# Four column tiles for three matrix-vector products of an attention and MLP training step

## The chip, the cores and the metric

One core of one Trainium2 chip runs the whole program in one launch. The metric is the device time of a run in microseconds (us), as a median over runs; lower is better. TensorE multiplies matrices (PE in the profile, PEld for its weight loads), VectorE (DVE) and ScalarE (ACT) work on rows and copy results out of PSUM, GpSimd (POOL) and SyncE (SP) here mostly issue transfers.

## The reference

One token, x of 1 x 1024, goes twice through attention and an MLP with the same weights, and then all gradients are computed with a given gradient of the output:

```
def _A_ref(x, k_cache, v_cache, wq, wo):        # 32 heads, 4 kv groups, head size 128, last 4096 positions
    q = (x @ wq).reshape(...)                   # wq 1024 x 4096
    p = softmax(q k^T * 128**-0.5)
    return (p v).reshape(B, Sq, 4096) @ wo      # wo 4096 x 1024
def _B_ref(x, w1, b1, w2):
    h = x @ w1 + b1                             # w1 1024 x 3584
    act = h * tanh(softplus(h))
    return act @ w2                             # w2 3584 x 1024
x = x + A(layernorm(x)); x = x + B(layernorm(x))
x = x + A(layernorm(x)); x = x + B(layernorm(x))
```

The outputs are x and the gradients of the first x, both caches, wq, wo, w1, b1 and w2, all bf16. The gradients of the caches (1 x 4 x 32768 x 128 each) are zero outside the last 4096 positions, and these zeros are written too.

## The kernel before

Vectors of 1024, 3584 or 4096 numbers are held as columns: 128 partitions by 8, 28 or 32 columns. A weight matrix comes from memory in chunks of 1 MB, in the slots of a ring of eight (`Ring`; `want` queues a load, `release` frees a slot and lets SP issue the next load that was wanted, `lend` adds slots). A forward product takes 128 x 128 blocks of a chunk as the stationary operand and one column of the vector as the moving operand, and adds up columns in PSUM. Backward products need the transposed matrix: TensorE transposes eight blocks at a time into a PSUM bank (`turn_pe`, L452), ACT or DVE copies them back over the chunk (`turn_ev`, `evac`, L305 and L308), and then the same form of product follows, put off by `later` until two or more such groups are under way (`mv`, L471). Part of the rows is done instead by DVE as dot products (`rowdot`, L429).

The order, with l = 0 and 1 for the two layers of each kind: attention 0, MLP 0, attention 1 (`attn_fwd`), the first half of MLP 1 (`mlp_fwd`); then backward through MLP 1 (`dn_b1`), attention 1 (`attn_bwd`), MLP 0, attention 0; at the end the outer products of the weight gradients and the cache gradients are computed and stored (`work`). The second MLP's output is not needed until the end, so its product with w2 (`mlp_out`, L697) is done on the way back, in the loop over w2's seven chunks in which the gradient of the first MLP also passes through w2 (`rows_chunk`). Engines follow the program's order; nothing is rescheduled.

What the change touches:

- In `attn_fwd`, the loop over wo's eight chunks (L596), 32 matmuls for each, with `wo_hook` after each chunk. In the second layer the hook does one `conv`: eight transposes of a block of the K cache and a copy, work for the backward pass. The result goes to `residual` (L387), and from there through a layernorm to the MLP.
- In `mlp_fwd`, the loop over w1 (L645), 224 matmuls, whose result `h_ps` goes to DVE (L658). W1 stays in SBUF.
- The loop over w2's chunks on the way back (from L1094), with `mlp_out` ahead of `rows_chunk`. Here a row group is transposed in two of four, and DVE takes the other two. After it follow `dn_b0`, which ends with `ring.lend`, and `attn_bwd(0, ...)`, whose hooks `do1(c)` run after each wo chunk.
- PSUM: SC0 and SC1, MV, TP and three BIG banks. Seven of eight banks are in use.

The zeros of the cache gradients go out as 56 transfers of 1 MB. `zeros(n, after)` issues n of them on POOL at points in the program that were chosen by hand; a tiny copy of `after` makes POOL wait until that value exists.

Of the kernel before, what the change touches and what calls it, by code (L numbers as in the profile page):

```python
# [9 lines left out]
FP32 = mybir.dt.float32  # L10
BF16 = mybir.dt.bfloat16
ACT = mybir.ActivationFunctionType
ALU = mybir.AluOpType
AX = mybir.AxisListType

P = 128
HQ = 32
# [6 lines left out]
TD = D // P  # L24
TF = F // P
# [68 lines left out]
def kernel(  # L94
# [22 lines left out]
    nc = tc.nc  # L117
# [10 lines left out]
    psum = way.enter_context(tc.tile_pool(name="psum", bufs=1, space=bass.MemoryType.PSUM))  # L128
    dram = ctx.enter_context(tc.tile_pool(name="dram", bufs=1, space=bass.MemoryType.DRAM))

    def sb(shape, dtype, name):
        return keep.tile(shape, dtype, name=name)
# [12 lines left out]
    W1 = sb([P, TD, F], BF16, "W1")  # L145
# [8 lines left out]
    small = junk[:].bitcast(FP32)  # L154

    mlp_t = DSX[:, 0:1024].bitcast(FP32)
# [4 lines left out]
    SC = [psum.tile([P, 512], FP32, name=f"SC{i}")[:] for i in range(2)]  # L161
    MV = psum.tile([P, 512], FP32, name="MV")
    TP = psum.tile([P, 512], FP32, name="TP")
    bigs = [psum.tile([P, 512], FP32, name=f"BIG{i}")[:] for i in range(3)]
    big_n = [0]

# [22 lines left out]

    spread = sb([P, P + 3], BF16, "spread")  # L190
    nc.vector.memset(spread[:], 0.0)
    quarter = sb([P, 4], FP32, "quarter")
    nc.vector.memset(quarter[:], 0.0)
    for hi in range(4):
# [6 lines left out]
    NB = sb([P, TD, 2], BF16, "NB")  # L201
    GA = sb([P, TD, 2], BF16, "GA")
    GB = sb([P, TD, 2], BF16, "GB")
    OC = sb([P, HQ, 2], BF16, "OC")
    DQC = sb([P, HQ, 2], BF16, "DQC")
    AC = sb([P, TF, 2], BF16, "AC")
# [13 lines left out]
    ring = Ring(nc, [ring_t[:, i, :] for i in range(8)])  # L220
# [115 lines left out]
    def f_block(row, b):  # L336

        c = b // 4
        return row[:, 512 * c:512 * (c + 1)].rearrange("a (p k) -> a k p", k=4)[:, b % 4, :]

    def into_fours(dst, col):

# [40 lines left out]
    def residual(y_ps, x, name):  # L383
        xn = sb([P, TD], FP32, f"x_{name}")
        st = tmp([P, 2], FP32, "st")
        junk = tmp([P, TD], FP32, "xx")
        nc.vector.scalar_tensor_tensor(out=xn[:], in0=y_ps, scalar=1.0, in1=x[:], op0=ALU.mult, op1=ALU.add,  # L387
                                       accum_out=st[:, 0:1])
        nc.vector.scalar_tensor_tensor(out=junk[:], in0=xn[:], scalar=1.0, in1=xn[:], op0=ALU.mult, op1=ALU.mult,
                                       accum_out=st[:, 1:2])  # L390
        return xn, st
# [110 lines left out]
    def attn_fwd(l, x, st, first, wo_hook, q_hook=None):  # L502
        name = f"A{l}"
# [7 lines left out]
        for k, t in enumerate(order):  # L511
            ch = ring.get(("q", l, t))
            for h in range(HQ):
                nc.tensor.matmul(q_ps[:, h:h + 1], lhsT=ch[:, h * P:(h + 1) * P], rhs=NA[:, t, l:l + 1],  # L514
                                 start=(k == 0 and h == 0), stop=(k == TD - 1), skip_group_check=True)
# [11 lines left out]
        for i in range(2):  # L527
            for t in range(16 * i, 16 * i + 16):
                for g in range(G):
                    c = scol(g, t) - 512 * i  # L530
                    nc.tensor.matmul(SC[i][:, c:c + 8], lhsT=KT[:, g, t, :],
                                     rhs=QC[:, 0, g * 32 + l * 8:g * 32 + l * 8 + 8], start=True, stop=True)
            nc.vector.reduce_max(m64[i][:], SC[i].rearrange("p (tp c) -> p c tp", c=64), axis=AX.X)
        if not first:
# [5 lines left out]
                                op=ALU.max)  # L540
# [20 lines left out]
        for i in range(2):  # L561
            nc.vector.reduce_sum(m64[i][:], EX[:, i * 512:(i + 1) * 512].rearrange("p (tp c) -> p c tp", c=64), axis=AX.X)
            for g in range(G):
                for t in range(16 * i, 16 * i + 16):
                    c = scol(g, t)
# [24 lines left out]
        y_ps = MV[:, 128:128 + TD]  # L590
        for c in range(8):
            ch = ring.get(("o", l, c))
            for tt in range(4):
                h = 4 * c + tt
                for dd in range(TD):
                    nc.tensor.matmul(y_ps[:, dd:dd + 1], lhsT=ch[:, tt, dd * P:(dd + 1) * P], rhs=OC[:, h, l:l + 1],  # L596
                                     start=(h == 0 and dd == 0), stop=(h == HQ - 1), skip_group_check=True)
            if first:
                ring.release(("o", l, c))
            wo_hook(c)  # L600
        xn, stn = residual(y_ps, x, name)
        return xn, stn, dict(n32=n32, rstd=rstd, o32=o32)

# [34 lines left out]
    def mlp_fwd(l, x, st, mid):  # L638
        name = f"B{l}"
        n32, rstd = ln_fwd(x, st, NB[:, :, l], name)  # L640
        mid()
        h_ps = MV[:, 192:192 + TF]
        for t in range(TD):
            for fb in range(TF):
                nc.tensor.matmul(h_ps[:, fb:fb + 1], lhsT=f_block(W1[:, t], fb), rhs=NB[:, t, l:l + 1],  # L645
                                 start=(t == 0 and fb == 0), stop=(t == TD - 1), skip_group_check=True)

        taken = []

        def col(n):  # L650
            if n == "mp":
                return sb([P, TF], FP32, f"{n}_{name}")
            taken.append(n)
            return mlp_t[:, (len(taken) - 1) * TF:len(taken) * TF]

        h, nh, z, w, m, om, A, B, num, den, t_, = (col(n) for n in "h nh z w m om A B num den t".split())
        V = nc.vector
        V.tensor_tensor(out=h[:], in0=h_ps, in1=b1c[:], op=ALU.add)  # L658

        V.scalar_tensor_tensor(out=nh[:], in0=h[:], scalar=-1.0, in1=h[:], op0=ALU.mult, op1=ALU.min)  # L660
        nc.scalar.activation(z[:], nh[:], ACT.Exp)
        nc.scalar.activation(w[:], nh[:], ACT.Exp, scale=2.0)
        V.tensor_scalar(out=m[:], in0=h[:], scalar1=0.0, scalar2=None, op0=ALU.is_ge)
        V.tensor_scalar(out=om[:], in0=h[:], scalar1=0.0, scalar2=None, op0=ALU.is_lt)
        V.tensor_tensor(out=A[:], in0=m[:], in1=w[:], op=ALU.max)
        V.tensor_tensor(out=B[:], in0=om[:], in1=w[:], op=ALU.max)
        V.scalar_tensor_tensor(out=num[:], in0=z[:], scalar=2.0, in1=A[:], op0=ALU.mult, op1=ALU.add)
        V.scalar_tensor_tensor(out=den[:], in0=B[:], scalar=2.0, in1=num[:], op0=ALU.mult, op1=ALU.add)
        V.reciprocal(den[:], den[:])
        V.tensor_tensor(out=t_[:], in0=num[:], in1=den[:], op=ALU.mult)  # L670
        if l == 0:
            V.tensor_tensor(out=AC[:, :, l], in0=h[:], in1=t_[:], op=ALU.mult)

        def deriv():

            mp, sg, s2 = col("mp"), col("sg"), col("s2")
            V.tensor_scalar(out=s2[:], in0=z[:], scalar1=1.0, scalar2=None, op0=ALU.add)
            V.reciprocal(s2[:], s2[:])
            V.tensor_tensor(out=sg[:], in0=m[:], in1=z[:], op=ALU.max)
            V.tensor_tensor(out=sg[:], in0=sg[:], in1=s2[:], op=ALU.mult)  # L680
            V.tensor_tensor(out=mp[:], in0=t_[:], in1=t_[:], op=ALU.mult)
            V.tensor_scalar(out=mp[:], in0=mp[:], scalar1=-1.0, scalar2=1.0, op0=ALU.mult, op1=ALU.add)
            V.tensor_tensor(out=mp[:], in0=mp[:], in1=h[:], op=ALU.mult)
            V.tensor_tensor(out=mp[:], in0=mp[:], in1=sg[:], op=ALU.mult)
            V.tensor_tensor(out=mp[:], in0=mp[:], in1=t_[:], op=ALU.add)
            return mp

        def act_late():
            V.tensor_tensor(out=AC[:, :, l], in0=h[:], in1=t_[:], op=ALU.mult)

        return dict(n32=n32, rstd=rstd, deriv=deriv, act_late=act_late)

    def mlp_out(l, ch, c, y_ps):
        for tt in range(4):
            fb = 4 * c + tt
            for dd in range(TD):
                nc.tensor.matmul(y_ps[:, dd:dd + 1], lhsT=ch[:, tt, dd * P:(dd + 1) * P], rhs=AC[:, fb, l:l + 1],  # L697
                                 start=(fb == 0 and dd == 0), stop=(fb == TF - 1), skip_group_check=True)
# [326 lines left out]
    def units_rows(base, nblk, out):  # L1025

        for c in range(nblk // 4):
            s = stage_free.popleft()
            for tt in range(4):
                n = 0  # L1030
                while n < 2:
                    m = unit_dw(base, NOFF + (4 * c + tt) * P, 512 * n, s[:, tt * D + n * 512:(tt + 1) * D], 2 - n)
                    n += m
                    store(out.rearrange("(c p k) d -> p c (k d)", p=P, k=4)[:, c], s, 2 * tt + n - m, 2 * tt + n, 8,
                          c == nblk // 4 - 1)
                    yield
# [64 lines left out]
    bigs.append(SC[1])  # L1101
    for c in range(7):
        ch = ring.get(("2", 1, c))
        mlp_out(1, ch, c, y_ps)
        flush()
        rows_chunk(ch, c, GB, 0, LB[0], da0, DA, 2 if c else 0, "A" if c else None, ("2", 1, c))
        later(lambda c=c: ring.release(("2", 1, c)))
        if c in (2, 4):
            zeros(1, da0[:, 4 * c:4 * c + 1])
# [9 lines left out]
    nc.vector.tensor_copy(GA[:, :, 0], g1[:])  # L1119

    x4 = sb([P, TD], BF16, "x4")
    nc.vector.tensor_tensor(out=x4[:], in0=y_ps, in1=x3[:], op=ALU.add)
    db = sb([P, TF], BF16, "db")
    nc.vector.tensor_tensor(out=db[:], in0=dh0[:], in1=dh1[:], op=ALU.add)

# [5 lines left out]
    def do1(c):  # L1131
        if c == 0:
            rowize(GA, TD, 32, 0)
        if c == 3:
            todo[1].append(units_rows(32, HQ, out_5))
        if c == 5:
            store_rows(x4[:], TD, out_0[0, 0, :])
            store_f(db)
        if c == 5:
            zeros(2, do1_acc[:, 4 * c:4 * c + 1])  # L1140
# [76 lines left out]
```

## Time and profile before

| | |
|---|---|
| median of 3 runs | 457.55 us (455.9 to 457.78) |
| profiled execution | 456.82 us, of which the span from first to last instruction is 455.0 us |
| mean granted TensorE clock | 0.641 |
| busy share of the span | PE 72%, PEld 58%, DVE 57%, ACT 46%, POOL 9% |
| DMA | 181.48 MB (81.84 MB read, 98.62 MB written from the HBM's side), mean 399 GB/s |
| attention 1, output product (L596) | 133.15 us to 145.99 us, when `residual` starts |
| MLP 1, first product (L645) | 149.16 us to 159.69 us, when its result is read |
| w2's loop on the way back | 252.25 us to 277.44 us |

Times inside the execution count from the start of the span. The page cuts the span into 40 equal slices and gives each engine's busy share as a digit in tenths; the line PEclk is the clock that the throttle granted to TensorE, in tenths of full speed with 9 for 90% or more; the line GB/s is what all DMA queues moved. A timeline line has start, length, engine, source line, operation, output and input, count, and in brackets the idle time before it with what ended it. Matmuls are pipelined: the length of a group of matmuls runs from the first start to the modelled end of the last.

### The profile page before, as it was taken

What the parts mean: (1) busy time and instruction counts of PE and PEld (TensorE: products, weight loads), DVE (VectorE), ACT (ScalarE), POOL (GpSimd) and SP (SyncE); (2) the same over time, 40 slices, a digit from 0 to 9 for tenths busy, and PEclk for the clock granted to TensorE, in tenths of its full rate; (3) what the DMA queues carried; (4) which work ended last, traced back from release to release, by engine and by line L of the source; (5) the groups of instructions that cost most, each with busy time, mean ns of one, the idle gap of its engine ahead of it and who ended that gap; (6) DMA issues with size and microseconds to landing.
All of it is one profiled execution on the core that took longest, in us unless ns stands there. A gap on an engine that the chain in (4) does not pass through costs nothing. (4 is left out here: it accounts for less than half of the span.)

```text
span 455.0 us, 14050 instructions
## 1 busy us (share of the span) xinstructions
PE 326.4 (72%) x6289; PEld 262.1 (58%) x6289; DVE 258.8 (57%) x508; ACT 210.6 (46%) x245; POOL 38.8 (9%) x86
## 2 busy tenths in 40 slices
PE   3836543456599788898797988798977898889500
PEld 3735443456598778797797877796861222235300
DVE  4504747277450075477366847486377999888600
ACT  2501001011055276687066452283349999999500
POOL 1000000002032221200210101012221000000000
PEclk9955555555555588999589655697675555555555
DMA  8999999989989999999999899999999999999996
GB/s 336 424 418 418 421 416 419 419 321 421 421 349 403 401 407 412 410 393 418 420 419 421 341 402 333 361 371 416 421 420 420 417 421 423 423 419 419 404 408 248
DMA packets 28091, 181.48 MB, mean 399 GB/s; under 512 B 3675, under 2 KB 3703, under 8 KB 9463
## 3 DMA queue, kind: packets, MB, share of 16 engines
q1 hardware_dynamic: 19874, 121.84, 66.1%
q0 software_dynamic: 8064, 58.72, 31.6%
q8 instruction: 49, 0.80, 0.7%
q14 instruction: 12, 0.09, 0.0%
q10 hardware_dynamic: 92, 0.02, 0.0%
HBM read 81.84 MB, written 98.62 MB: 397 GB/s over the span
## 5 line engine op out<-in xcount | busy, mean ns | idle before, releaser
L308 ACT COPY ring<-BIG 128x1024 bf16<-128x1024 bf16 x51 | 50.5, 1015 | 44.0 <-PE BIG L452 37.6
L1019 PE MATMUL wide<-W 2*128 2x512 bf16 x228 | 52.1, 598 | 9.3 <-ACT W L308 2.0
L452 PE MATMUL BIG<-ident_bf,ring 128*128 128x128 bf16 x664 | 55.5, 238 | 1.4 <-ACT ring L308 0.4
L452 PEld LDWEIGHTS <-ring 128*128 128x128 bf16 x768 | 53.2, 109 | 2.4 <-issue 1.7
L429 DVE CUSTOM_DVE_ANT_0 junk<-ring,SC 128x1024 bf16<-128x1024 bf16 x32 | 38.9, 1215 | 6.7 <-DMA ring<-in_B_w_dram 6.2
L1019 PEld LDWEIGHTS <-W 2*128 2x128 bf16 x240 | 12.6, 102 | 44.3 <-issue 43.2
L471 PEld LDWEIGHTS <-ring 128*128 128x128 bf16 x864 | 29.9, 97 | 10.5 <-issue 6.8
L305 DVE CAST ring<-wide 128x1024 bf16<-128x1024 f32 (+1 forms) x29 | 33.7, 1200 | 3.2 <-PE wide L1019 1.5
L308 ACT COPY KT<-BIG 128x1024 bf16<-128x1024 bf16 x22 | 21.9, 1011 | 27.5 <-PE BIG L625 26.0
L308 ACT CAST ring<-wide 128x1024 bf16<-128x1024 f32 (+1 forms) x35 | 32.9, 1018 | 1.3 <-PE wide L1070 0.5
L305 DVE COPY ring<-BIG 128x1024 bf16<-128x1024 bf16 x32 | 21.8, 689 | 16.6 <-PE BIG L452 12.7
L264 POOL DMA_DIRECT2D out_dram<-zt x56 | 29.7, 534 | 15.0 <-DMA out_dram<-zt 14.2
L429 DVE CUSTOM_DVE_ANT_0 junk<-ring,DSX 128x1024 bf16<-128x1024 bf16 x24 | 29.4, 1224 | 0.8
L645 PE MATMUL MV<-NB,W 128*128 128x1 bf16 x448 | 16.5, 172 | 15.5 <-DMA W<-in_B_w_dram 12.7
L645 PEld LDWEIGHTS <-W 128*128 128x128 bf16 x448 | 15.8, 118 | 16.3 <-DMA W<-in_B_w_dram 13.4
L452 PE MATMUL BIG<-ident_bf,W 128*128 128x128 bf16 x288 | 23.3, 227 | 2.4 <-issue 2.4
L514 PE MATMUL MV<-NA,ring 128*128 128x1 bf16 x512 | 15.2, 165 | 13.1 <-DMA ring<-in_A_wq_dram 11.8
L308 ACT COPY W<-BIG 128x1024 bf16<-128x1024 bf16 x21 | 20.6, 1015 | 7.9 <-PE BIG L452 7.4
L514 PEld LDWEIGHTS <-ring 128*128 128x128 bf16 x512 | 14.6, 103 | 13.9 <-DMA ring<-in_A_wq_dram 12.4
L305 DVE CAST VS<-wide 128x1024 bf16<-128x1024 f32 (+1 forms) x17 | 19.7, 1187 | 3.6 <-PE wide L1019 3.0
L1070 PE MATMUL wide<-W 32*128 32x256 bf16 x128 | 20.9, 402 | 0.9 <-ACT ring L308 0.6
L308 ACT CAST KT<-wide 128x1024 bf16<-128x1024 f32 x20 | 20.4, 1032 | 1.8 <-PE wide L1019 0.9
(258 smaller groups left out, 551.5 us busy)
## 6 DMA issues: line engine op xcount, KB each, us to landing
out_dram<-zt POOLq DMA_DIRECT2D x56, 1024.0 KB, 15.1
ring<-in_A_wq_dram SPq DMA_DIRECT2D x24, 1024.0 KB
ring<-in_A_wo_dram SPq DMA_DIRECT2D x14, 1024.0 KB
ring<-in_B_w_dram SPq DMA_DIRECT2D x13, 1024.0 KB
W<-in_A_wo_dram SPq DMA_DIRECT2D x10, 1024.0 KB
W<-in_B_w_dram SPq DMA_DIRECT2D x8, 896.0 KB
out_dram<-ring SPq DMA_DIRECT2D x7, 1024.0 KB
out_dram<-ring SPq DMA_DIRECT2D x13, 512.0 KB
```

The costliest lines, as they stand in the source:

```text
L264: nc.gpsimd.dma_start(dst, zt[:])
L305: nc.vector.tensor_copy(dst, src)
L308: nc.scalar.copy(dst, src)
L429: nc.vector.tensor_tensor_reduce(out=out, in0=a, in1=vec, scale=1.0, scalar=acc if i else 0.0, op0=ALU.mult, op1=ALU.add, accum_out=acc)
L452: nc.tensor.transpose(b[:, i * P:(i + 1) * P], block(w, i) if block else w[:, i * P:(i + 1) * P], ident_bf[:])
L471: nc.tensor.matmul(out, lhsT=w[:, i * P:(i + 1) * P], rhs=rhs_of(i), start=fresh[0], stop=last and i == n - 1, skip_group_check=True)
L514: nc.tensor.matmul(q_ps[:, h:h + 1], lhsT=ch[:, h * P:(h + 1) * P], rhs=NA[:, t, l:l + 1], start=(k == 0 and h == 0), stop=(k == TD - 1), ...
L645: nc.tensor.matmul(h_ps[:, fb:fb + 1], lhsT=f_block(W1[:, t], fb), rhs=NB[:, t, l:l + 1], start=(t == 0 and fb == 0), stop=(t == TD - 1), ...
L1019: nc.tensor.matmul(b[:, 512 * i:512 * i + 512], lhsT=R[at:at + 2, lo:lo + P], rhs=R[at:at + 2, ro + 512 * i:ro + 512 * i + 512], start=Tru ...
L1070: nc.tensor.matmul(b[:, k * 256:(k + 1) * 256], lhsT=RT[32 * g:32 * g + 32, a, tp, :], rhs=YS[32 * g:32 * g + 32, :], start=True, stop=Tru ...
```

## The change

Three products turn their operands round: the second attention layer's output product, the second MLP's first product, and the second MLP's output product on the way back. The vector's column, repeated 32 times, becomes the stationary operand (128 x 32), and 512 columns of the weight matrix stream past it. Four such products sit beside each other on the four column tiles of the array, and write to partitions 0, 32, 64 and 96 on of one PSUM bank. The result then lies as rows, in partial sums for the two products with wo and w2; it is copied to SBUF and turned back into columns by small f32 matmuls against `sel4` or `sel2`, which pick one partition of each 32 and add the partial sums. A new bank YR holds the rows of the first and third product; the second uses SC0 and SC1. The third is turned back only in the fifth chunk (c == 4) of the last `attn_bwd` loop, and the sum `x4`, which was formed right after `dn_b0`, moves there too.

```
+    YR = psum.tile([P, 512], FP32, name="YR")
...
+    sel4 = sb([P, 4], FP32, "sel4")
+    nc.vector.memset(sel4[:], 0.0)
+    sel2 = sb([P, 2], FP32, "sel2")
+    nc.vector.memset(sel2[:], 0.0)
+    for j in range(4):
+        nc.vector.memset(sel4[32 * j:32 * j + 1, j:j + 1], 1.0)
+        nc.vector.memset(sel2[32 * j:32 * j + 1, j % 2:j % 2 + 1], 1.0)
...
+    def row_mm(bank, j, stat, mov, first, last):
+        nc.tensor.matmul(bank[32 * j:32 * j + 32, :], lhsT=stat.to_broadcast([P, 32]), rhs=mov, start=first, stop=last,
+                         skip_group_check=True, tile_position=(0, 32 * j))
+    def rows_by_two(bank, ch, c, n, vec):
+        for tt in range(4):
+            k = 4 * c + tt
+            for s in range(2):
+                row_mm(bank, 2 * (k % 2) + s, vec(k), ch[:, tt, 512 * s:512 * s + 512], k < 2, k >= n - 2)
+    def two_to_cols(bank, buf, out):
+        ov = out.rearrange("p (s i) -> p i s", s=2)
+        for h in range(2):
+            nc.vector.tensor_copy(buf[:, 256 * h:256 * h + 256], bank[:, 256 * h:256 * h + 256])
+            for i in (2 * h, 2 * h + 1):
+                nc.tensor.matmul(ov[:, i, :], lhsT=buf[:, i * P:(i + 1) * P], rhs=sel2[:], start=True, stop=True,
+                                 skip_group_check=True)
...  attn_fwd
             ch = ring.get(("o", l, c))
+            if not first:
+                rows_by_two(YR, ch, c, HQ, lambda h: OC[:, h, l:l + 1])
+                wo_hook(c)
+                continue
...
+        if not first:
+            two_to_cols(YR, small, y_ps)
         xn, stn = residual(y_ps, x, name)
...  mlp_fwd
+        if l == 0:
...
+        else:
+            for t in range(TD):
+                for c in range(7):
+                    row_mm(SC[c // 4], c % 4, NB[:, t, l:l + 1], W1[:, t, 512 * c:512 * c + 512], t == 0, t == TD - 1)
+            hv = [h_ps[:, 0:16].rearrange("p (j k) -> p k j", k=4), h_ps[:, 16:28].rearrange("p (j k) -> p k j", k=4)]
+            for b, (buf, copy) in enumerate(((small, nc.vector.tensor_copy), (mlp_t, nc.scalar.copy))):
+                n = 32 * (4, 3)[b]
+                copy(buf[0:n, :], SC[b][0:n, :])
+                bv = buf[0:n, :].rearrange("p (m k) -> p k m", k=4)
+                for k in range(4):
+                    nc.tensor.matmul(hv[b][:, k, :], lhsT=bv[:, k, :], rhs=sel4[0:n, 0:n // 32], start=True, stop=True,
+                                     skip_group_check=True)
...  the loop over w2's chunks on the way back
-        mlp_out(1, ch, c, y_ps)
+        rows_by_two(YR, ch, c, TF, lambda fb: AC[:, fb, 1:2])
...  after dn_b0
-    nc.vector.tensor_tensor(out=x4[:], in0=y_ps, in1=x3[:], op=ALU.add)
...  do1(c)
+        if c == 4:
+            two_to_cols(YR, RT.rearrange("p a t s -> p (a t s)")[:, 0:1024].bitcast(FP32), y_ps)
+            nc.vector.tensor_tensor(out=x4[:], in0=y_ps, in1=x3[:], op=ALU.add)
         if c == 5:
             store_rows(x4[:], TD, out_0[0, 0, :])
```

More of the change, by code (lines that the diff above doesn't have):

```diff
@@ L597, in attn_fwd @@
                                      start=(h == 0 and dd == 0), stop=(h == HQ - 1), skip_group_check=True)
-            if first:
-                ring.release(("o", l, c))
+            ring.release(("o", l, c))
             wo_hook(c)
+        if not first:
+            two_to_cols(YR, small, y_ps)
         xn, stn = residual(y_ps, x, name)
@@ L642, in mlp_fwd @@
         h_ps = MV[:, 192:192 + TF]
[L643 to L646, printed above, removed]
+        if l == 0:
+            for t in range(TD):
+                for fb in range(TF):
+                    nc.tensor.matmul(h_ps[:, fb:fb + 1], lhsT=f_block(W1[:, t], fb), rhs=NB[:, t, l:l + 1],
+                                     start=(t == 0 and fb == 0), stop=(t == TD - 1), skip_group_check=True)
+        else:
+            for t in range(TD):
+                for c in range(7):
[8 more added lines that the diff above has]
+                                     skip_group_check=True)
         taken = []
```

## The prediction

> **What bounds the kernel now.** I read the page's slices first, then stretches of 5 us, then the timeline of the three stages that change. The slices (11.4 us each):
>
> ```profile
> PE   3836543456599788898797988798977898889500
> ...
> PEclk9955555555555588999589655697675555555555
> DMA  8999999989989999999999899999999999999996
> GB/s 336 424 418 418 421 416 419 419 321 421 421 349 403 401 407 412 410 393 418 420 419 421 341 402 333 361 371 416 421 420 420 417 421 423 423 419 419 404 408 248
> ```
>
> TensorE has nothing in the last two slices, and DMA still moves over 400 GB/s there: the last instruction of an engine ends near 428.5 us and the queues drain until about 452 us. So the end is set by DMA: 181.48 MB at some 410 GB/s. Compute that gets faster is worth only what DMA idles less. From the first changed product (133 us) on, DMA falls short in one region, seen in 5 us stretches (start:end, length, busy us of PE, PEld, DVE, ACT, POOL, granted clock, DMA share, GB/s):
>
> ```profile
> 250.00:255.00 5.00, 4.23 (x99) 3.73 (x97) 3.49 (x10) 1.30 (x2) 0.71 (x2) 0.96 0.97 395
> 255.00:260.00 5.00, 4.83 (x113) 4.75 (x110) 4.86 (x9) 2.65 (x3) 0.70 (x2) 0.50 0.74 264
> 260.00:265.00 5.00, 4.83 (x101) 4.75 (x99) 2.56 (x6) 3.19 (x4) 0.00 (x0) 0.50 1.01 411
> 265.00:270.00 5.00, 3.79 (x87) 3.44 (x85) 2.33 (x5) 2.59 (x3) 0.70 (x2) 0.50 1.01 383
> 270.00:275.00 5.00, 4.40 (x87) 4.13 (x85) 3.65 (x7) 1.93 (x2) 0.00 (x0) 0.50 1.02 400
> 275.00:280.00 5.00, 3.39 (x80) 2.96 (x79) 1.98 (x9) 1.93 (x2) 1.25 (x3) 0.50 0.98 354
> 280.00:285.00 5.00, 4.47 (x127) 4.05 (x125) 4.42 (x14) 1.25 (x2) 0.00 (x0) 0.50 0.95 315
> 285.00:290.00 5.00, 3.19 (x51) 3.19 (x51) 1.28 (x10) 0.19 (x1) 0.00 (x0) 0.50 0.92 344
> 290.00:295.00 5.00, 4.61 (x65) 4.20 (x64) 2.90 (x8) 2.42 (x4) 0.00 (x0) 0.78 0.99 359
> ```
>
> Two measures of the shortfall: the missing share, 0.03+0.26+0.02+0.05+0.08+0.01 of 5 us, is 2.3 us; the missing bytes against 410 GB/s (15+146+27+10+56+95+66+51 = 466 GB/s over 5 us) are 5.7 us. The cause of the deepest hole is in the timeline of SP's queue: w2's chunk 4 can be asked for only when chunk 0's slot is released (256.23 us), and by then the four chunks in hand and the zeros issued up to 251.88 us have all moved. The dips at 278 to 283 and 288 to 292 us are of the same kind: the next reads wait for `ring.lend` (issued at 287.61 us), after the stage and `dn_b0`. So a lead X of compute over its old clock at 250 us turns into time, about one for one, until the holes are full: between 2.3 and 5.7 us. A lag deepens them in the same way. After 303 us DMA has work in hand to the end.
>
> **What a row product costs.** The old form is cheap: in the timeline 32 matmuls with one moving column take 1.06 us of weight loads (33 ns each; 34 in B). The new one sends 512 columns. No row shows column tiles with so many. The transposes give the pace of a column: 128 columns in 1.62 us / 16 = 101 ns at clock 0.5 and 0.46 us / 8 = 57 ns at clock 1.0, so 512 columns take about 405 or 230 ns. If four tiles run side by side that is 101 or 57 ns each, if they go one after the other 405 or 230. The nearest rows are matmuls of 512 columns in two row groups, at clock 0.5, and the one use of column tiles (8 columns, `into_fours`):
>
> ```profile
> 345.82 3.36 PE L1019 MATMUL wide<-W 2*128 2x512 bf16 x14 [0.67 <-ACT VS L308]
> ...
> 132.39 0.34 PE L348 MATMUL TP<-junk,ident_bf 128*32 128x8 bf16 x16
> ...
> 132.67 0.10 PEld L596 LDWEIGHTS <-ring 128*128 128x128 bf16 x1
> ```
>
> 14 in 3.36 us is 240 ns each, near half of 405: parts of the array do run side by side. I take four. The clock: 24 transposes back to back from 159.79 us lifted it from 0.5 to 1.0 by 163 us, and in 195 to 215 us transposes mixed with single columns at some 60% kept it. Single columns don't lift it, nor do the 2-partition matmuls of the last stage. Four full-height tiles resemble the transposes, so I take clock 1.0 after 3 us.
>
> The third line bears on switching forms: weights for a full-width matmul load at 132.67 us while the column-tile matmuls still run (to 132.73 us), so leaving costs nothing visible; entering costs at most the 0.20 us that PEld waits there for issue. [...]
>
> **A, second output product (256 matmuls to 64).** Before it runs from 133.15 us to `residual` at 145.99 us: 12.8 us, one chunk and one `conv` every 1.70 us. After, two chunks at clock 0.5 (16 x 101 ns = 1.6 us, one conv 0.72 us), then six chunks of 8 x 57 ns = 0.46 us with a conv of 0.48 us: the last row product is at about 141.4 us. The tail is new and in the open: a DVE copy of 256 columns (512 float columns take 0.69 us in L896; I say 0.42), two f32 matmuls (two of L572 take 0.93 us at clock 0.5, one of L408 0.30 us at 1.0), the second copy under them, two more, semaphores: 1.9 us, 2.4 us cold. End 143.3 us: 2.7 us earlier. Wholly at clock 0.5 it is 8 x 0.81 + 7 x 0.72 + 2.4 - 0.7 = 13.6 us, 0.7 later. `residual` waits on DVE for the matmuls, and nothing that others need stands behind it. The ACT copies of the convs (1.01 us each) keep up.
>
> **B, second MLP's first product (224 to 56).** Before 149.16 to 159.69 us, 10.5 us, of which 2.8 us is a wait for issue in the middle. After: 3 us cold (28 row products), 28 x 57 ns = 1.6 us, then in the open the two copies side by side (DVE 0.69 us), eight f32 matmuls (0.30 to 0.47 us each: 2.4 to 3.8) and semaphores: 7.9 to 9.2 us. All cold 5.7 + 4.7 = 10.4 us. So 1.3 to 2.6 us earlier, cold 0.1. The three products go from 704 matmuls to 176 and 16 in f32, so TensorE is fed fewer instructions and I count no issue wait; if it stays, B's gain is gone.
>
> X is then 2.7 + 2.0 = 4.7 us; I take 4, for switches of tiling (15 of 0 to 0.2 us). Between 164 and 250 us nothing changes, and reads land well ahead, so the lead is kept.
>
> **C, w2's product on the way back (224 to 56).** Removing TensorE work here is worth little by itself, because the period of 3.31 us is a ring of dependences:
>
> ```profile
> 259.33 1.01 PE L452 MATMUL SC<-ident_bf,ring 128*128 128x128 bf16 x8
> 260.43 1.01 ACT L308 COPY ring<-SC 128x1024 bf16<-128x1024 bf16 x1 [1.39 <-issue]
> 261.33 1.02 ACT L308 COPY ring<-BIG 128x1024 bf16<-128x1024 bf16 x1
> 262.40 0.29 PEld L471 LDWEIGHTS <-ring 128*128 128x128 bf16 x8 [0.25 <-ACT ring L308]
> 262.62 1.62 PEld L452 LDWEIGHTS <-ring 128*128 128x128 bf16 x16
> ```
>
> Eight transposes (1.03 us to their end), two ACT copies (1.93 us), the product that reads the second, then the next transposes. TensorE already waits 0.25 us for ACT in it. Taking out 1.06 us and putting 0.46 to 0.81 us in lengthens that wait and nothing else, unless the clock rises: the transposes then end in 0.61 us, 0.4 us less per chunk, 2.8 us over seven. Chunks 5 and 6 also waited for DMA (1.3 and 0.9 us), which the lead shortens. I count C at 0 to 2.8 us of further lead, and need none of it.
>
> **Edits at nothing.** The memsets of `sel4` and `sel2` lie in DVE's wait for the first inputs (3.9 us). YR takes the one bank that was free. The four f32 matmuls at c == 4 of the last output product sit in TensorE's queue behind two DVE copies, and `x4` on DVE behind the matmuls; the transposes and row dots of that loop wait behind both. The copies also wait on three SP transfers (small row transfers, issued at about this loop's start). Cost 1.5 to 3 us of compute. The cover: some 1.5 MB more than was needed is in DMA's hands at 311.78 us, 3.7 us, and the lead; without it, up to 3 us. `out_0` still leaves at c == 5.
>
> **The sum.** X of 4 us lets chunk 4 be asked for at 252.2 us instead of 256.23, while DMA is still busy; chunk 6 then lands near 264 us instead of 272.6, the stage ends near 271 instead of 277.4 us, `ring.lend` falls near 281 us, and what is in hand until then (zeros and wo's first chunks) lasts to about 283 us. Nearly all holes close: between 2.3 and 5.7 us, I take 4.0, the middle. From the profiled execution's 456.82 us that is 452.8; it lies 0.7 us under the median of the runs, so I forecast a median of 453.5 us.
>
> **Rivals.** *No lead:* the clock stays at 0.5, or only two tiles run side by side, or the issue wait of B comes back. Cold, A is 0.7 us later and B 0.1 earlier; with pairs (115 ns warm) A is 1 and B 0.6 us later; with the issue wait alone X is A's gain less a little. X from -1.6 to +1: the holes 1 us shallower to 1.6 us deeper, a median of 456.5 to 459.2 us. For it: clock 0.5 is what the trace shows from 22 to 160 us. Against: the transposes at 160 us.
>
> *One at a time (slower):* the four tiles don't overlap, 230 ns each after 3 us. A: 3.0 + 56 x 0.23 + 7 x 0.48 + 1.8 = 21.1 us, 8.2 longer; B: 3.0 + 48.6 x 0.23 + 3.4 = 17.6, 7 longer; X = -15. The zeros before 196 us (27 MB from 133.7 us) last to about 199.5 us, 3.5 us more than needed; so 11.5 us: a median of 469 us. It decides from where four row products take over about 0.5 us warm. Against it: the 240 ns above, and loads of 109 ns that overlap transposes of 238 ns on the same rows. [...]
>
> **How the numbers follow.** Forecast 0.60 (of it 0.06 within 0.5%), no lead 0.25 (0.17 within, 0.04 faster, 0.04 slower), one at a time 0.12 and other delays 0.03, both slower. 0.5% is 2.3 us, about what a measurement of this kernel can tell from no change. Faster 0.54 + 0.04 = 0.58, within 0.23, slower 0.19. The range goes from 450.5 (holes of 5.7 us closed and a good 1 us of mixing besides) to 460 (no lead, its worst end): left out are the one-at-a-time case and little else.
>
> **What would show it.** Right: row products starting 55 to 110 ns apart at clock 1.0 in A and B; `residual` near 143, the stage of C starting near 248 us; 255 to 295 us at 390 GB/s or more; the last engine instruction well ahead of the last transfer. Wrong: row products over 200 ns apart, f32 tails over 5 us, or a lead that arrives with the holes still there, which would say that they aren't starved of requests.

## The result, and the profile after

The change gives a median of 455.33 us (20 runs) against 457.85 us (20 runs) of the kernel before: a ratio of 0.9941 (95% interval 0.9922 to 0.9960), 0.6% faster. One run of the change, of 465.0 us at a granted clock of 0.565, was in a slower state of the chip and is left out of the ratio. The forecast was a median of 453.5 us, so 4 us of gain where 2.5 to 2.7 came. The profiled execution took 455.47 us (span 453.7 us), 1.35 us less than the one before; single executions of one kernel lie some 4 us apart, so the traces show where time goes, and the repeated runs how much.

The slices of the page after:

```profile
PEclk9955555555559879599679955788585555555555
DMA  8999999989989999999999999999999999999996
GB/s 333 422 423 417 420 418 420 416 313 423 418 363 397 406 407 408 409 392 417 423 422 420 363 387 355 359 411 395 423 413 417 413 416 421 416 422 414 406 408 268
```

The granted clock is up in the thirteenth slice (the second output product, 136 us on) and mixed behind it: in the seventeenth, 181 to 193 us, the digit is 5 where it was 9 before. DMA still sets the end (the last instruction of an engine ends at 428.1 us, the span at 453.7 us), and the dips between 250 and 310 us are there, a little shallower. The stretches that answer to those of the prediction (same columns; those left out have shares of 0.97 and more, and 403 to 418 GB/s but for 356 at 265 us):

```profile
255.00:260.00 5.00, 4.07 (x76) 2.70 (x73) 3.98 (x8) 3.40 (x4) 0.70 (x2) 1.00 0.86 311
...
275.00:280.00 5.00, 3.69 (x110) 3.39 (x108) 3.05 (x11) 0.86 (x2) 1.24 (x3) 0.50 1.00 346
280.00:285.00 5.00, 3.09 (x86) 2.80 (x84) 3.13 (x10) 1.00 (x1) 0.00 (x0) 0.50 0.96 340
285.00:290.00 5.00, 5.00 (x76) 5.00 (x73) 2.77 (x13) 1.01 (x1) 0.00 (x0) 0.54 0.82 288
```

The hole at 255 us went from a share of 0.74 to 0.86; the one at 285 us got deeper (0.92 to 0.82). Over 250 to 310 us DMA moved 373 GB/s instead of 364, which is 0.54 MB or 1.3 us: as much as the two profiled executions differ.

The first changed product, in the timeline (start, length, engine, line, operation, output and inputs, count, idle before):

```profile
133.13 1.90 PE L351 MATMUL YR<-ring,OC 128*32 128x512 bf16 x16 [0.32 <-DVE OC L379]
...
137.05 0.61 PE L351 MATMUL YR<-ring,OC 128*32 128x512 bf16 x8
137.60 0.62 PE L659 MATMUL BIG<-ident_bf,KT 128*128 128x128 bf16 x8
138.15 0.61 PE L351 MATMUL YR<-ring,OC 128*32 128x512 bf16 x8
...
142.59 1.05 PE L367 MATMUL MV<-sel,junk 128*128 128x2 f32 x8
```

Sixteen products in 1.9 us at clock 0.5, then eight and eight transposes in a period of 1.10 us at clock 1.0: the four tiles do run side by side. Eight products and the switches on both sides take 1.10 less eight transposes of 57 ns, 0.64 us. If a product takes 57 ns too, 0.18 us is left for the two changes of tiling, an estimate of 0.09 us each; 56 products without a change between them took 3.63 us at clock 1.0 in a later run (dense_turn), 65 ns each with the end of the last one included. `residual` starts at 143.68 us (145.99 before).

The second product:

```profile
145.87 5.32 PE L351 MATMUL SC<-W,NB 128*32 128x512 bf16 x56 [0.90 <-DVE NB L403]
...
151.77 2.03 PE L692 MATMUL MV<-sel,junk 128*128 128x4 f32 x8 [0.59 <-DVE junk L689]
153.66 2.01 PE L692 MATMUL MV<-sel,DSX 96*128 96x3 f32 x8
```

Its result is read at 155.78 us (159.69 before): a lead of 3.9 us. The clock fell back to 0.5 by 147 us and was at 1.0 again from 150 us, so some 3.4 us of the 5.3 were spent at the lower one. The trace lists each f32 matmul as two (x8 for the first product's four), so the eight take 3.9 us, 0.49 us each, though the granted clock is 1.0 there; the four of the first product took 1.05 us, 0.25 each, at clock 1.0 too.

### The profile page after: what moved, and what is told of

Its sections match the earlier page's. It is cut to its first block, busy times and chain, and to the rows that moved or that the text cites. A ratio compares the mean times of both kernels' runs of the same rounds, so it can differ in the third digit from the quotient of the medians.

```text
span 453.7 us, 13076 instructions
## 1 busy us (share of the span) xinstructions
PE 327.4 (72%) x5793; PEld 251.3 (55%) x5793; DVE 261.9 (58%) x523; ACT 211.4 (47%) x246; POOL 38.7 (9%) x86
## 5 line engine op out<-in xcount | busy, mean ns | idle before, releaser
L481 PE MATMUL BIG<-ident_bf,W 128*128 128x128 bf16 x288 | 24.6, 235 | 2.9 <-issue 2.9
L481 PEld LDWEIGHTS <-W 128*128 128x128 bf16 x288 | 19.4, 115 | 3.3 <-issue 3.3
L500 PEld LDWEIGHTS <-W 128*128 128x128 bf16 x480 | 16.6, 101 | 3.6 <-issue 2.2
```

What stands on the lines that cost most here:

```text
L481: nc.tensor.transpose(b[:, i * P:(i + 1) * P], block(w, i) if block else w[:, i * P:(i + 1) * P], ident_bf[:])
L500: nc.tensor.matmul(out, lhsT=w[:, i * P:(i + 1) * P], rhs=rhs_of(i), start=fresh[0], stop=last and i == n - 1, skip_group_check=True)
```

## The experiments

Theory L: what turns into time is compute's lead over DMA, which fills holes where DMA has nothing in its queues. All ratios are to the kernel before, on the same chip, with 95% intervals.

**Which product gives the gain.** Four kernels hold one or two of the three parts; the others are in the old form.

a_only, the second output product alone (in `mlp_fwd` `if l == 0:` becomes `if True:`, and the loop on the way back calls `mlp_out`):

> Only the second output product on column tiles. Both theories: residual about 2.3 us earlier than before, as in the profile of the change (143.68 against 145.99 us). Theory L (the time comes from compute's lead at 250 us filling DMA's holes, wherever the lead was made): some of it is left at 250 us, 0.5 to 1.5 us; time 0.1 to 0.3% below before. Theory C (the time comes from the product inside the hole, w2's on the way back, and the lead of the two earlier products is lost on the way): within 0.1% of before.

b_only, the second MLP's first product alone (`if not first:` ahead of `rows_by_two` becomes `if False:`):

> Only the second MLP's first product on column tiles. Both theories: its result is read about 1.5 us earlier than before. Theory L: 0.1 to 0.3% below before, less than 1 us of lead left at 250 us. Theory C: within 0.1% of before.

c_only, w2's product on the way back alone:

> Only w2's forward product on the way back on column tiles, turned back at c == 4. Theory L: nothing earlier than 252 us; the pace of the first chunks falls from 3.3 to about 2.9 us if the granted clock stays at 1.0, and the time is 0 to 0.2% below before. Theory C: the whole gain, 0.4 to 0.7% below before.

ab, the first two:

```
-        rows_by_two(YR, ch, c, TF, lambda fb: AC[:, fb, 1:2])
+        mlp_out(1, ch, c, y_ps)
```

> Both early products on column tiles, w2's as before. Theory L: most of the change's gain, 0.3 to 0.6% below before. Theory C: within 0.2% of before.

Measured: a_only 0.9963 (0.9940 to 0.9986), b_only 0.9986 (0.9961 to 1.0012), c_only 0.9992 (0.9963 to 1.0021), ab 0.9937 (0.9911 to 0.9964). The first two together give what the whole change gives, the third gives nothing that can be measured: theory C falls. a_only's 0.37% is a little more than theory L had for it. b_only alone can't be told from no change.

In a_only's trace the second product's result is read at 155.61 us, as early as in the change (155.78), with that product in its old form: the first product and the layernorm behind it at a risen clock (0.87 over 136 to 150 us instead of 0.50; 2.2 us for the layernorm instead of 3.2) make nearly the whole lead. In b_only's trace (an execution of 459.9 us; the median is 456.77) it is read at 160.07 us, not 1.5 us earlier than before but 0.4 later: the output product ahead of it, in its old form, waited 1.95 us for issue, where it had waited 0.56.

**Is it the lead?** after_delay is the change with six copies in the path behind the second product, so that TensorE's stream stays and the lead goes:

```
         V.tensor_tensor(out=h[:], in0=h_ps, in1=b1c[:], op=ALU.add)
+        if l == 1:
+            for _ in range(6):
+                V.tensor_copy(small, SC[0])
```

> The change, and behind the second MLP's first product six copies of 0.69 us each on DVE in the path: 4.1 us of delay with the same TensorE stream as the change. Theory L (compute's lead over DMA is what turns into time): the lead of 3.9 us at the end of that product is gone, the time is back within 0.2% of before. Rival S (the gain is from the shorter and differently clocked TensorE stream after 160 us, not from the lead): the time stays 0.4 to 0.7% below before.

Measured: 1.0017 (0.9988 to 1.0045). In its trace `dh1` is ready at 163.49 us, as before the change (163.70), and the gain is gone. The column tiles and the shorter stream as such give nothing. Two limits: the granted clock is another one too (150 to 165 us 0.70 against 0.77 in the change, 165 to 190 us 0.90 against 0.81), and the profiled execution, 456.29 us for a median of 457.86, has later marks near the change's (`ring.lend` at 287.04 against 287.34 us), so the repeated runs show the loss and this trace doesn't show where. big_lead goes the other way:

```
-            for tt in range(4):
+            for tt in range(4 if first or c == 0 else 0):
...
-        for t in range(TD):
+        for t in range(TD if l == 0 else 1):
```

> The kernel before, with most of two products left out: of the second output product only the first of eight chunks, of the second MLP's first product only the first of eight row blocks; the outputs are not the reference's. It makes a lead of 14 to 16 us without column tiles. Theory L: the holes of 250 to 310 us fill until they are full: 2.3 to 5.7 us below before, 0.5 to 1.2%, not 14 us. If the lead were lost on the way whatever its size (clock, issue waits): no more than the change's 0.6%.

Measured: 0.9920 (0.9890 to 0.9950). `g3` comes 11.3 us earlier than before (176.95 against 188.28 us) and `g2` 11.8 us earlier (239.85 against 251.64), yet the time falls by 0.8%, 3.7 us: the gain saturates, inside the 2.3 to 5.7 us that was expected. But it doesn't saturate because the holes are full. Up to 280 us they are (419 to 428 GB/s); behind that a deeper one has opened:

```profile
280.00:285.00 5.00, 4.61 (x84) 4.31 (x83) 3.03 (x6) 2.47 (x5) 0.00 (x0) 0.90 0.59 231
285.00:290.00 5.00, 3.74 (x101) 3.65 (x97) 3.67 (x7) 3.82 (x4) 0.00 (x0) 1.00 0.84 283
```

```profile
279.05 5.79 SPq L825 DMA_DIRECT2D W<-W  x2
284.95 1.37 SPq L71 DMA_DIRECT2D W<-in_A_wo_dram  x3
```

The second line of the second view is `ring.lend`, at 284.95 us only 2.7 us earlier than before. SP has two row transfers to issue ahead of it and waits 4.3 us between them, by the trace for a read of wo; why so long stays open. A lead of 8.3 us at the end of w2's loop (`dh0` at 269.63 us, 277.96 before) is 2.7 us there. So 3.7 us is what this lead brought, not what the holes hold.

**Are the holes dry queues?** zeros_before and zeros_after pull three zero transfers forward, on the kernel before and on the change:

```
-    zeros(1, g2)
+    zeros(2, g2)
...
-    zeros(2, dh0)
+    zeros(4, dh0)
```

> The kernel before, with one zero transfer more at g2 (2 for 1) and two more at dh0 (4 for 2), taken from the last ones. Theory H (the holes at 255 to 258 and 278 to 292 us are queues that have run dry): they take 3.1 MB, 2 to 4 us below before, 0.4 to 0.9%, with the products as they were. Rival R (more zeros take bandwidth from w2's and wo's reads there, chunks land later and the holes move behind): within 0.3% of before.

> The change, with the same three zero transfers moved. Theory H: the holes that the change leaves (0.82 of DMA at 285 to 290 us, 0.86 at 255 to 260 us) fill too: 1 to 3 us below the change, 0.8 to 1.2% below before. Rival R: within 0.3% of the change.

Measured: zeros_before 0.9942 (0.9919 to 0.9965), zeros_after 0.9926 (0.9900 to 0.9952). Three MB moved forward in the old kernel give as much as the whole change, with no faster product. Two of the stretches in zeros_before's trace, which had a share of 0.74 and 0.92 (264 and 344 GB/s) before:

```profile
255.00:260.00 5.00, 4.44 (x132) 4.29 (x132) 4.86 (x9) 2.94 (x3) 0.71 (x2) 1.00 1.00 369
285.00:290.00 5.00, 3.18 (x60) 3.12 (x57) 1.49 (x9) 0.09 (x1) 0.00 (x0) 0.50 1.01 421
```

Over 250 to 310 us it moves 390 GB/s instead of 364. The reads behind do come later, as rival R has it (`ring.lend` at 291.84 us, 287.61 before), but the time falls all the same: the holes are dry queues, and rival R falls on the kernel before. On top of the change theory H misses: 0.15% (0.7 us) less than the change's ratio where 1 to 3 us were expected, inside the 0.3% that rival R allows, and intervals overlap. In zeros_after's trace 250 to 310 us moves 398 GB/s (373 in the change), but new holes open behind it: 371 and 366 GB/s at 335 to 345 us and 345 at 350 to 355 us, where the change has 407, 416 and 418. The zeros that were moved forward are missing there.

**The f32 matmuls of the second product.** dense_turn lets the two copies write the rows in the order of the columns:

```
-                copy(buf[0:n, :], SC[b][0:n, :])
-                bv = buf[0:n, :].rearrange("p (m k) -> p k m", k=4)
+                copy(buf[0:n, :].rearrange("p (k m) -> p k m", k=4), SC[b][0:n, :].rearrange("p (m k) -> p k m", k=4))
+                bv = buf[0:n, :].rearrange("p (k m) -> p k m", k=4)
```

> The change, with the second MLP's rows put in the order of the columns by the two copies, so that its eight f32 weight loads read neighbouring columns and not every fourth. Theory P (the stride of 16 bytes is what makes one such matmul 0.49 us there against 0.25 us in the first product's tail, both at granted clock 1.0): eight take about 2.0 us and not 3.9, the copies stay within 0.2 us, the lead grows by about 1.8 us, the time is 0.1 to 0.3% below the change, 0.6 to 0.9% below before. Theory Q (it is the clock in that moment, not the stride): 3.5 us or more for the eight, time as the change's.

```profile
150.53 0.69 DVE L689 COPY junk<-SC 128x512 f32<-128x512 f32 x1 [3.20 <-PE SC L351]
...
151.28 1.05 PE L692 MATMUL MV<-sel,junk 128*128 128x4 f32 x8 [0.59 <-DVE junk L689]
152.19 1.03 PE L692 MATMUL MV<-sel,DSX 96*128 96x3 f32 x8
```

Theory P holds for the step: 0.25 us each, the copy as before, `dh1` at 157.40 us instead of 159.88. Of these 2.5 us the f32 matmuls are 1.9; besides, in this execution the clock stayed at 1.0 through the 56 products (3.63 us instead of 5.32), and the output product ended 1.2 us later. The time did not follow: 0.9964 (0.9944 to 0.9985), where 0.6 to 0.9% below before was expected, and no better than the change. Its profiled execution (457.71 us; the median is 455.6) has its deepest dips at 265 to 285 us and 295 to 305 us.

**Holes earlier, and all together.** early_zeros issues two zero transfers behind the second attention's exponentials; all_with_c has those, the ordered copies and the three zeros moved; all_no_c is the same with w2's product in the old form:

```
         if not first:
             conv_ev(late, "A")
+            zeros(2, EX)
```

> The kernel before, with two zero transfers issued behind the second attention's exponentials (about 127.5 us), taken from the last ones. Theory H: they fill the hole of 132 to 136 us (missing share 0.27 + 0.59 + 0.80, 1.7 us), 0.3 to 0.4% below before. Rival R: wo's chunks, still landing, come later and hold up the second output product: within 0.2% of before.

> The change with the ordered copies, the two early zeros, one more at g2 and two more at dh0. Theory H: the gains of the holes add, 1.0 to 1.4% below before, 451 to 453 us. If the holes are one budget that any filler uses up: 0.7 to 0.9%.

> As the last one, with w2's product on the way back in its old form. Theory L (that product is in a ring of dependences and gives nothing): within 0.2% of the run with it. If it does give something when the clock stays up: that run is 0.2 to 0.5% faster than this.

Measured: early_zeros 0.9965 (0.9946 to 0.9985), the size that theory H has; all_no_c 0.9895 (0.9866 to 0.9925), median 452.62 us, the best kernel of the study; all_with_c 0.9962 (0.9941 to 0.9982).

The gain of early_zeros is not shown to come from the hole alone. The hole is full (415 GB/s in 130 to 136 us, 304 before), but in its trace TensorE's waits for issue in the two forward products, 0.56 and 2.76 us before, are gone as well, with both products in their old form. `dh1` comes 4.5 us earlier (159.20 us for the cast against 163.67): a lead larger than the change's, from an edit that touches no product. Where these waits come from is open; between 133 and 160 us they sum to 2.3 to 4.9 us in the traces of before, a_only, b_only, c_only and zeros_before and to nothing in the other nine. `ring.lend` then comes late (293.12 us, 287.61 before), again behind 4.3 us that SP waits between the two row transfers, and 290 to 295 us moves 53 GB/s.

Neither all_with_c nor all_no_c came out as any theory had it: the gains do not add in the first, and the second is faster than the first, not slower. So the third part of the change, which gives nothing in the change, costs 0.67% here. Two views of all_with_c show where. Stretches of 60 and 5 us:

```profile
250.00:310.00 60.00, 40.52 (x698) 35.57 (x695) 29.35 (x67) 20.29 (x23) 3.52 (x8) 0.61 1.00 417
345.00:350.00 5.00, 3.68 (x56) 2.03 (x56) 3.98 (x15) 2.58 (x6) 0.00 (x0) 0.59 0.69 282
350.00:355.00 5.00, 3.42 (x17) 0.77 (x17) 2.26 (x4) 4.30 (x8) 0.00 (x0) 0.50 0.17 69
```

The holes of 250 to 310 us are full (417 GB/s against 364 before). But a new one opens at 345 us, where the kernel before has 419 and 422 GB/s. The reading is that the zeros which used to bridge the time until the first gradients are stored were spent earlier, that compute then sets the end, and that each delay in the last `attn_bwd` counts. The timeline of that loop in all_with_c:

```profile
299.41 1.03 PE L481 MATMUL BIG<-ident_bf,W 128*128 128x128 bf16 x8 [5.22 <-DMA W<-in_A_wo_dram]
...
306.40 0.75 DVE L365 COPY W<-YR 128x256 f32<-128x256 f32 x2 [2.88 <-DMA W<-W]
306.88 1.87 PE L367 MATMUL MV<-sel,W 128*128 128x2 f32 x8 [3.89 <-DVE W L365]
308.78 0.17 DVE L1185 TENSOR_TENSOR x<-MV,x_A 128x8 bf16<-128x8 f32 x1 [1.63 <-PE MV L367]
```

The copy out of YR waits 2.88 us on DVE for a small row transfer that stands in SP's queue behind the wo chunks; TensorE waits 3.89 us behind it, DVE 1.63 us more for the f32 matmuls. all_no_c has none of these three waits (the 5.22 us for a wo chunk in the first line it has too, as 4.71), and moves more: its hole at 345 us is a little smaller (97 and 321 GB/s in the same two stretches), and all_with_c has dips at 310 and 320 us besides (277 and 300 GB/s in 5 us, 369 and 423 there), which are most of the difference. That the waits are the cause rests on these two traces; no run took away the wait alone.

## Why the prediction was right, point by point

- **The bound and the holes: right.** DMA ends the kernel, and between 250 and 310 us it runs dry. zeros_before shows the second by filling them with other transfers. That a lead turns into time until the holes are full is not shown: big_lead's 3.7 us lie inside the 2.3 to 5.7, but a hole behind 280 us stayed, and in its trace `ring.lend` stands behind SP's row transfers, which the prediction left out.
- **Four side by side at a clock that rises: right.** 16 in 1.9 us at clock 0.5 where one at a time would be 6.5 us, and at clock 1.0 the period above. A change of tiling costs an estimated 0.09 us, inside the 0 to 0.2 us given. One at a time is refuted, and *no lead* too: the lead at the second product's end was 3.9 us, the X of 4 that was taken.
- **A: right** (143.68 for 143.3 us). **B: 9.9 us for 7.9 to 9.2**, only 0.6 us less than before. X came out all the same, by luck in part, because the layernorm between the two, at clock 1.0 instead of 0.5, took 2.2 us instead of 3.2 (it ends at 145.87 for 149.16 us), which wasn't counted. Two of B's terms were too small. The 56 products took 5.2 us to the first copy for 4.6. The eight f32 matmuls took 3.9 us for 2.4 to 3.8: their price came from matmuls with weights side by side; here they lay 16 bytes apart, at 0.49 us each for the 0.25 us of dense_turn, which lays them side by side, both at clock 1.0. No wait for issue is left between 133 and 160 us, as predicted, but fewer instructions need not be the reason, since early_zeros has none either. One sum is wrong: A wholly at clock 0.5, by its own terms, is 13.2 us and not 13.6, so 0.4 us later than before and not 0.7, in a rival that did not come about.
- **C: right.** The clock stayed at 1.0 until 262 us and the first chunks came every 2.25 to 2.9 us, and then they waited for DMA:

```profile
258.82 0.61 PE L351 MATMUL YR<-ring,AC 128*32 128x512 bf16 x8
263.40 1.04 PE L351 MATMUL YR<-ring,AC 128*32 128x512 bf16 x8 [1.62 <-DMA ring<-in_B_w_dram]
267.47 1.04 PE L351 MATMUL YR<-ring,AC 128*32 128x512 bf16 x8 [0.78 <-DMA ring<-in_B_w_dram]
```

- **"Between 164 and 250 us nothing changes ... so the lead is kept": wrong, and the likely reason that 2.5 to 2.7 us came and not 4.** In the profiled executions the lead is 3.8 us at `dh1`, 2.1 at `g3`, 0.7 at the first wq request, 0 at the first w2 request and 1.2 at `g2`. Chunk 4 was asked for at 255.17 us, not 252.2 (256.23 before); the stage of C ended at 276.1 us, not 271, and `ring.lend` fell at 287.34 us, not 281. In the traces it isn't the waits for issue, which sum to the same (6.7 us before and 6.9 us after from 160 us to the first w2 request). What differs is the granted clock; before the change, and after it:

```profile
180.00:185.00 5.00, 4.65 (x83) 4.49 (x82) 2.66 (x5) 3.00 (x4) 0.00 (x0) 0.70 1.01 415
185.00:190.00 5.00, 3.91 (x63) 3.42 (x63) 1.61 (x12) 3.80 (x5) 1.66 (x4) 1.00 1.01 419
```

```profile
180.00:185.00 5.00, 4.71 (x69) 4.55 (x67) 1.32 (x6) 2.84 (x4) 0.00 (x0) 0.54 1.01 415
185.00:190.00 5.00, 4.73 (x43) 4.35 (x44) 1.74 (x7) 2.86 (x5) 2.27 (x5) 0.50 1.02 410
```

  The layernorm step there took 3.7 us instead of 2.3 (from `dn` to `g3`), and the first transposes behind it ran at half clock; at 230 to 232 us, too, the clock was 0.60 instead of 0.81. This was read, not tested: dense_turn, with 6.3 us of lead at `dh1`, kept 2.7 at `g2` and was no faster than the change, and the profile of ab has no lead at `g2` (252.12 us) in an execution of 455.06 us. ab's DMA gains behind 290 us (412 and 391 GB/s in two stretches of 10 us, 374 and 375 before), after a `dn_b0` without the wait for issue of 2.34 us that the kernel before has there. The lead at one mark of one trace doesn't rank kernels. What is shown is that without the lead the gain is nil; at which place the lead becomes time is open.
- **Edits at nothing: right in the change, with the cover that was named.** There the copy at c == 4 did not wait, and the f32 matmuls took 1.05 us. In all_with_c, without the cover, it waited as described, for 2.88 us on DVE and 3.89 on TensorE where up to 3 us was given.

## What to carry to other kernels

Where the end is set by transfers, ask first where their queues run dry and what the next request waits for; count the lead of a faster step only so far as it gets there (here 3.9 us at the second product's end gave 2.5 to 2.7 us of time); moving an independent transfer into the hole may be worth as much (0.6% here with two numbers changed). Independent transfers are a budget: spent early, they were missing here where they used to bridge a gap (282 and 69 GB/s at 345 to 355 us in all_with_c, 419 and 422 before), and then, by the reading of two traces, waits that had been covered counted. An edit that costs nothing under cover should be tried again once the cover is used up. And before a gain is put down to an edit, compare the marks ahead of it: with two transfers meant to fill a hole, compute stood 4.5 us earlier in the trace as well.

## What was not expected of the hardware

- f32 weights 16 bytes apart took 0.49 us for a 128 x 128 matmul with 3 or 4 moving columns, those side by side 0.25 us, both at granted clock 1.0. What lies behind the factor of two is not shown.
- Four column tiles with 128 rows and 512 columns lifted the granted clock, as 24 transposes did in the kernel before (0.50 up to 162 us, 0.76 in the next, 1.00 from 163 us, after a start at 159.79 us). In the change's second product, with nothing else on TensorE from 145.87 us on, it was 0.50 from 147 to 149 us, 0.66 in the next and 1.00 from 150 us. The old form, single columns, left it at 0.50 in the kernel before from 149.16 to 153.3 us, with TensorE busy all that time.
